# Which output tiles lend their buffers to the last two output pairs of a sliding-window attention and soft-MoE kernel

## The chip, the cores and the metric

The kernel runs on one core of one Trainium2 chip. The metric is device time in microseconds; before the change the median of 8 runs is 182.9 us (182.35 to 183.49).

A core has several engines that work side by side, each with its own queue of instructions in order: TensorE (PE, matmuls), VectorE (DVE), ScalarE (ACT), GpSimd (POOL) and SyncE (SP). The last two matter here mainly because they issue DMA transfers. An engine waits at the head of its queue until what its next instruction needs is there; whatever stands behind it waits too. The bytes of all transfers are moved by 16 DMA engines.

## The reference

An attention over 8 batches, 8 heads, 576 positions and head size 64 feeds a soft mixture of experts. Four heads see a plain window of 32 positions, the other four a window of 128 positions of which every fourth counts. The attention's result, 4608 rows of 512, is the input x of the mixture:

```python
logits = x @ phi                        # 4608 x 32 (8 experts x 4 slots)
d = softmax of logits over the rows     # dispatch
slot_input = d.T @ x                    # 32 x 512
h = relu(slot_input[e] @ w1[e])         # for each expert e, its 4 slots: 4 x 1024
slot_out[e] = h @ w2[e]                 # 4 x 512
c = softmax of logits over the slots    # combine
out = c @ slot_out                      # 4608 x 512, float32
```

The change lies in the last line alone: out = c @ slot_out and its way to memory.

## The kernel before

The attention and the statistics of the mixture run batch by batch, in an order written out by hand. At the end of that part the exponentials of all logits stand in a tile ET, with the 32 slots along the partitions, and the weights of the experts come in by DMA as the last input. The second part computes the experts and then the output.

**The output** is made in 36 blocks of 128 rows (NFIN), taken two at a time as 18 pairs. A block is one matmul of ET's columns with slot_out (so_sb), into a PSUM tile f; then ACT or DVE multiplies each row by the reciprocal of its sum of exponentials (rrow) on the way to an SBUF tile; then a DMA writes that to the output in device memory. There are three kinds of tile:

- *Halves*: pairs 0 to 7 are made in two column halves of 256 each, function `combine(half, pair)`. "Half 4" in this text is the second column half (half 1) of pair 4, "half 5" that of pair 5. An even pair is scaled by two ACT instructions (L774), an odd one by one DVE instruction (L778). The tile is float16, and POOL issues its DMA (L784), which casts to float32.
- *Full pairs* 8 to 15, `combine_full(pair)`: all 512 columns; the first block is scaled by ACT (L803), the second by DVE (L807), float16, and POOL issues the DMA (L814).
- *Full pairs* 16 and 17: the same, but scaled into float32, so that the DMA casts nothing, and it is SP that issues it (L814).

**Buffers.** SBUF is nearly full here, so some tiles take over a buffer that an earlier tile has held. The pool out_pool gives tiles of one tag the same buffers in turn; with one buffer to a tag, the next tile of that tag may be written when the DMA that reads the former one has landed. Seven second halves have buffers of their own under the tag ot1 (`bufs=NSPLIT // 2 - half`, 7). Two tags, last0 and last1, have one buffer each, of 128 x 2 x 512 float32. Before the change:

- last0: full pair 15 (float16, in the front of the buffer), then full pair 16
- last1: half 5 (float16, in the front of the buffer), then full pair 17

So the first instruction of full pair 16 (ACT, L803) waits until full pair 15's output has landed, and that of full pair 17 until half 5's has.

**Order.** The order of the instructions on every engine is the order in which the program writes them down (`manual_schedule`): full pairs 8 to 15, from pair 10 on each followed by one half (full 10, half 0, ... full 14, half 4, full 15, half 5), then halves 6 and 7, then full pairs 16 and 17. POOL's queue of issues is the same list up to half 7; SP's holds only pairs 16 and 17.

Of the kernel before, what the change touches and what calls it, by code (L numbers as in the profile page):

```python
# [9 lines left out]
FP32 = mybir.dt.float32  # L10
# [14 lines left out]
DMODEL = H * D  # L25
# [16 lines left out]
NFIN = N_ROWS // 128  # L42
# [7 lines left out]
def kernel(  # L50
# [607 lines left out]
    out_pool = tc.alloc_tile_pool(name="outp", bufs=1)  # L658
# [75 lines left out]
    def combine_one(half, blk):  # L734
        fp = psum_f.tile([128, NH], FP32, name=f"f{half}_one{blk}", tag="f")
        cols = slice(NH * half, NH * half + NH)
        r0 = 128 * blk
        nc.tensor.matmul(fp, ET[:, r0 : r0 + 128], so_sb[:, cols], start=True, stop=True)
        ot = out_pool.tile([128, NH], FP16, name=f"oo{half}_{blk}", tag=f"oo{half}_{blk}")
        if blk % 2 == 0:  # L740
            nc.scalar.activation(out=ot, in_=fp, func=AF.Copy, scale=rrow[:, blk : blk + 1])
        else:
            nc.vector.tensor_scalar(
                out=ot, in0=fp, scalar1=rrow[:, blk : blk + 1], scalar2=None, op0=ALU.mult
            )
        nc.gpsimd.dma_start(out=out[r0 : r0 + 128, cols], in_=ot)

    def combine(half, pair):
        if half == 0 and pair == 0:
            combine_one(half, 0)  # L750
            combine_one(half, 1)
            return
        fp = psum_f.tile([128, 2, NH], FP32, name=f"f{half}_{pair}", tag="f")
        r0 = 256 * pair
        for k in range(2):
            nc.tensor.matmul(
                fp[:, k, :],
                ET[:, r0 + 128 * k : r0 + 128 * k + 128],
                so_sb[:, NH * half : NH * half + NH],
                start=True,  # L760
                stop=True,
                skip_group_check=True,
            )
        if (half, pair) == (1, 5):
            ot = out_pool.tile([128, 2, DMODEL], FP32, name="last1_a", tag="last1")
            ot = ot[:, 0, 0:NH].bitcast(FP16).rearrange("p (k n) -> p k n", k=2)
        else:
            ot = out_pool.tile(
                [128, 2, NH], FP16, name=f"ot{half}_{pair}", tag=f"ot{half}", bufs=NSPLIT // 2 - half
            )  # L770
        if pair % 2 == 0:
            for k in range(2):
                blk = 2 * pair + k
                nc.scalar.activation(  # L774
                    out=ot[:, k, :], in_=fp[:, k, :], func=AF.Copy, scale=rrow[:, blk : blk + 1]
                )
        else:
            nc.vector.tensor_tensor(  # L778
                out=ot,
                in0=fp,  # L780
                in1=rrow[:, 2 * pair : 2 * pair + 2, None].broadcast_to([128, 2, NH]),
                op=ALU.mult,
            )
        nc.gpsimd.dma_start(  # L784
            out=out[r0 : r0 + 256, NH * half : NH * half + NH].rearrange("(k p) n -> p k n", k=2),
            in_=ot,
        )

    def combine_full(pair):
        r0 = 256 * pair  # L790
        if pair < NFIN // 2 - 3:
            ot = out_pool.tile([128, 2, DMODEL], FP16, name=f"of_{pair}", tag="of", bufs=6)
        else:
            tag = "last1" if pair == NFIN // 2 - 1 else "last0"
            ot = out_pool.tile([128, 2, DMODEL], FP32, name=f"ol_{pair}", tag=tag)
            if pair == NFIN // 2 - 3:
                ot = ot[:, 0, :].bitcast(FP16).rearrange("p (k n) -> p k n", k=2)
        for k in range(2):
            blk = 2 * pair + k
            fp = psum_f.tile([128, DMODEL], FP32, name=f"f_{blk}", tag="f")  # L800
            nc.tensor.matmul(fp, ET[:, 128 * blk : 128 * blk + 128], so_sb, start=True, stop=True)  # L801
            if k == 0:
                nc.scalar.activation(  # L803
                    out=ot[:, k, :], in_=fp, func=AF.Copy, scale=rrow[:, blk : blk + 1]
                )
            else:
                nc.vector.tensor_scalar(  # L807
                    out=ot[:, k, :],
                    in0=fp,
                    scalar1=rrow[:, blk : blk + 1],  # L810
                    scalar2=None,
                    op0=ALU.mult,
                )
        (nc.gpsimd if pair < NFIN // 2 - 2 else nc.sync).dma_start(  # L814
            out=out[r0 : r0 + 256, :].rearrange("(k p) n -> p k n", k=2), in_=ot
        )

    with tc.manual_schedule(engines=None):
        slot_out(0, ORDER[:6])
        slot_out(1, ORDER[:6])  # L820
        slot_out(0, HALVED)
        at = {5: 0}
        for pair in range(NSPLIT // 2):
            combine(0, pair)
            if pair in at:
                slot_out(1, (HALVED[at[pair]],))
        slot_out(1, HALVED[1:])
        for pair in range(NSPLIT // 2, NFIN // 2 - 2):
            combine_full(pair)
            if pair >= NFIN // 2 - NSPLIT // 2:  # L830
                combine(1, pair - (NFIN // 2 - NSPLIT // 2))
        for pair in range(2):
            combine(1, NSPLIT // 2 - 2 + pair)
        for pair in range(2):
            combine_full(NFIN // 2 - 2 + pair)
# [36 lines left out]
```

The softmax here doesn't subtract the row's maximum and nothing guards it: scores larger than these inputs give would overflow.

## Time and profile before

| what | value |
|---|---|
| median of 8 runs | 182.9 us (182.35 to 183.49) |
| the profiled execution, whole time | 183.03 us |
| its span, first to last instruction | 181.3 us |
| PE busy | 146.2 us (81%) |
| DVE, ACT, POOL busy | 107.3, 90.8, 83.7 us |
| the chain that ended last | DMA 41%, PE 34%, ACT 6%, POOL 6%, DVE 6% |
| read from and written to device memory | 61.93 MB, 9.44 MB |
| SP's two output transfers | 512 KB each, 1.05 MB together |

A profile comes from one execution. Its times count from the start of the span, in microseconds. The rows of digits cut the span into 40 equal slices, and a digit is the busy share in tenths. The row GB/s is what the 16 DMA engines moved. A line of the timeline has a start, a duration, the engine, the source line, the operation with the tiles it writes and reads, and in brackets how long the engine had been idle and what ended that. Tile names lose their numbers in it: `ol` is any of full pairs 15, 16 and 17, `ot` a half, `of` a full pair up to 14, and `last_a` is the half that sits in one of the two shared buffers. A row of a stretch has its length, the busy time (and the number of instructions) of PE, weight loads, DVE, ACT and POOL, then TensorE's clock, the DMA engines' mean busy share (over 1 where an engine has more than one packet in flight) and GB/s.

### The profile page before, as it was taken

To read this page: it belongs to the slowest core of one execution; us is meant where nothing else is said; L and a number is where in the kernel's file an instruction comes from. 1 tells how busy PE (TensorE), PEld (TensorE's weight loads), DVE (VectorE), ACT (ScalarE), POOL (GpSimd) and SP (SyncE) were. 2 spreads that over 40 slices of the span, in tenths; PEclk is the share of its full clock that TensorE was granted. 3 is DMA by queue.
4 is the path that set the end of the run, shared out by engine and by line. 5 is a ranking of instruction groups with operands and counts; after the bars stand their busy time and mean duration, and the time that the engine had idled before them with its cause. 6 is when DMAs were issued, how large, how long until landed. Compare 5 with 4: busy or idle time off the path is not lost.

```text
span 181.3 us, 5591 instructions
## 1 busy us (share of the span) xinstructions
PE 146.2 (81%) x2464; PEld 87.6 (48%) x2464; DVE 107.3 (59%) x232; ACT 90.8 (50%) x162; POOL 83.7 (46%) x124
## 2 busy tenths in 40 slices
PE   0467978999999999999999999998987986588000
PEld 0134445746655665664674674674735363233000
DVE  4689685876757676587598598443604024388030
ACT  2044454748555484765765765765430125497020
POOL 7954473633624163261444346334410443989700
PEclk9999995798589789789999999999755699889855
DMA  4999999999999999999999999999999999999996
GB/s 66 191 192 209 207 210 213 203 211 214 201 211 215 203 211 215 202 214 211 203 212 213 203 216 217 209 213 214 213 216 212 199 194 174 337 364 409 407 336 231
DMA packets 29527, 40.75 MB, mean 225 GB/s; under 512 B 1856, under 2 KB 19264, under 8 KB 29504
## 3 DMA queue, kind: packets, MB, share of 16 engines
q0 software_dynamic: 28960, 39.36, 116.1%
q1 hardware_dynamic: 544, 1.05, 1.6%
q8 instruction: 19, 0.31, 0.6%
q14 instruction: 4, 0.03, 0.0%
HBM read 61.93 MB, written 9.44 MB: 394 GB/s over the span
## 4 chain that ended last, share of the span: by engine, by line
DMA 41%; PE 34%; ACT 6%; POOL 6%; DVE 6%; issue 4%; DVEq 0%; POOLq 0%
DMA w<-in_moe_w_dram 28%; DMA raw<-in_k_dram 9%; ACT p L293 5%; PE lg L408 5%; PE o_p L339 4%; PE sa L282 4%; DMA out_dram<-ol 4%; PE sb L271 4%; PE sa L271 4%; PE rd L389 2%; DVE qk L245 2%; PE vb L163 2%; PE va L163 2%; PE u L452 2%; PE f L801 2%
## 5 line engine op out<-in xcount | busy, mean ns | idle before, releaser
L293 ACT ACTIVATE p<-sa 128x960 f16<-128x960 f32 (+2 forms) x24 | 21.4, 890 | 33.9 <-PE sb L282 33.3
L339 PEld LDWEIGHTS <-p 128*128 128x128 f16 (+2 forms) x544 | 19.7, 99 | 13.2 <-issue 9.0
L245 DVE STREAM_TRANSPOSE qk<-raw 128x320 uint32<-128x320 uint32 (+1 forms) x32 | 21.6, 679 | 0.3
L271 PE MATMUL sa<-masks,ident 128*128 128x480 f16 (+2 forms) x48 | 15.6, 414 | 7.3 <-POOL masks L489 6.2
L293 ACT ACTIVATE p<-sb 128x960 f16<-128x960 f32 (+2 forms) x24 | 21.2, 885 | 0.0
L236 DVE STREAM_TRANSPOSE qk<-raw 128x576 uint32<-128x576 uint32 x16 | 19.8, 1248 | 1.9 <-DMA raw<-in_k_dram 1.4
L271 PEld LDWEIGHTS <-ident 128*128 128x128 f16 x96 | 9.6, 112 | 18.9 <-issue 7.7
L282 PEld LDWEIGHTS <-qk 32*128 32x128 f16 x832 | 12.6, 101 | 12.0 <-issue 9.8
L408 PE MATMUL lg<-xTd,phi 128*128 128x288 f16 x32 | 18.3, 659 | 0.0
L339 PE MATMUL o_p<-v,p 128*128 128x65 f16 (+1 forms) x288 | 16.6, 202 | 1.2 <-ACT v L172 0.7
L282 PE MATMUL sa<-qk 32*128 32x160 f16 (+4 forms) x416 | 16.5, 218 | 0.8 <-DVE qk L236 0.7
L282 PE MATMUL sb<-qk 32*128 32x160 f16 (+4 forms) x416 | 16.5, 218 | 0.0
L209 POOL COPY v<-v 32x1024 f16<-32x1024 f16 x8 | 8.3, 1033 | 17.4 <-PE sb L282 10.3
L271 PE MATMUL sb<-masks,ident 128*128 128x480 f16 (+2 forms) x48 | 15.5, 411 | 0.5 <-ACT p L293 0.5
L212 POOL DMA_DIRECT2D w<-in_moe_w_dram x16 | 8.9, 556 | 14.6 <-DMA vs<-in_v_dram 6.6
L361 DVE TENSOR_TENSOR xp<-o_p,rc_p 128x448 f16<-128x448 f32 (+1 forms) x24 | 14.4, 602 | 0.9
L361 DVE TENSOR_TENSOR xd<-o_d,rc_d 128x448 f16<-128x448 f32 (+1 forms) x24 | 14.4, 602 | 0.8
L219 POOL DMA_DIRECT2D w<-in_moe_w_dram x10 | 6.7, 671 | 14.1 <-DMA w<-in_moe_w_dram 7.7
L412 ACT ACTIVATE ET<-lg 128x288 f16<-128x288 f32 x16 | 6.6, 410 | 12.6 <-PE lg L408 12.5
L163 PE MATMUL va<-vs,orders 32*128 32x256 f16 (+1 forms) x96 | 12.1, 290 | 0.9 <-ACT p L293 0.8
L360 DVE RECIPROCAL rc_p<-o_p 128x7 f32<-128x7 f32 (+1 forms) x24 | 4.7, 196 | 12.1 <-PE o_p L339 11.6
L382 ACT COPY xTp<-rp 128x576 f16<-128x576 f16 x16 | 10.4, 648 | 2.2 <-PE rp L377 2.2
(108 smaller groups left out, 277.8 us busy)
## 6 DMA issues: line engine op xcount, KB each, us to landing
w<-in_moe_w_dram POOLq DMA_DIRECT2D x16, 512.0 KB, 16.5
w<-in_moe_w_dram POOLq DMA_DIRECT2D x5, 1024.0 KB, 19.6
vs<-in_v_dram POOLq DMA_DIRECT2D x8, 512.0 KB, 14.3
raw<-in_q_dram POOLq DMA_DIRECT2D x7, 576.0 KB, 16.8
raw<-in_k_dram POOLq DMA_DIRECT2D x7, 576.0 KB, 17.1
out_dram<-ot POOLq DMA_DIRECT2D x14, 256.0 KB, 4.0
out_dram<-of POOLq DMA_DIRECT2D x7, 512.0 KB, 4.9
w<-in_moe_w_dram POOLq DMA_DIRECT2D x8, 256.0 KB, 9.6
```

Source lines behind the costliest of these rows:

```text
L163: nc.tensor.matmul(o.rearrange("p (h d) -> p h d", h=4), l, st[:, 0:4, D * r : D * r + D], start=(r == 0), stop=(r == DIL - 1), skip_group ...
L209: nc.gpsimd.tensor_copy(out=vL[b % NV][0:32, :, :, 0:D], in_=vD[b % NV][96:128, :, :, 0:D])
L212: nc.gpsimd.dma_start(out=w1t[e][:, 2 * i : 2 * i + 2, :].rearrange("p l f -> p (l f)"), in_=moe_w1[e, 256 * i : 256 * i + 256].rearrange( ...
L236: nc.vector.transpose(out=dst, in_=src)
L245: nc.vector.transpose(out=o, in_=i)
L271: nc.tensor.matmul(sps[h // 2][:, h % 2, 0:n], ident, bias[g], start=True, stop=False, skip_group_check=True,)
L282: nc.tensor.matmul(sps[h // 2][:, h % 2, c0 : c0 + w], kt_[32 * h : 32 * h + 32, k0 : k0 + 128, tt], qt_[32 * h : 32 * h + 32, q0 : q0 + w ...
L293: nc.scalar.activation(out=pt, in_=sps[ab][:, :, 0:n], func=AF.Exp, scale=SCALE)
L339: nc.tensor.matmul(o[p0 : p0 + np_, n, :], l, rr, start=(k == 0), stop=(k == len(jobs) - 1), skip_group_check=True,)
L361: nc.vector.tensor_tensor(out=x.rearrange("p t (h d) -> p (t h) d", h=4)[0:nq, u0:u1, :], in0=o[0:nq, 0:n, 0:D], in1=rc[0:nq, 0:n, None].b ...
L382: nc.scalar.copy(out=xTp_t[b][:, c, :], in_=rg)
L408: nc.tensor.matmul(lp, phi4[:, kc].rearrange("p c s -> p (c s)"), rhs, start=(kc == 0), stop=(kc == 3))
```

## The change

Half 4, not half 5, is put into one of the two shared buffers, and the tags of the full pairs are exchanged to match. After it:

- last0: half 4, then full pair 16
- last1: full pair 15, then full pair 17

Half 5 gets an ordinary buffer of the tag ot1, of which still seven are used. Nothing else differs: the order of instructions on each engine, their shapes and their number are the same.

```diff
-        if (half, pair) == (1, 5):
-            ot = out_pool.tile([128, 2, DMODEL], FP32, name="last1_a", tag="last1")
+        if (half, pair) == (1, 4):
+            ot = out_pool.tile([128, 2, DMODEL], FP32, name="last0_a", tag="last0")
             ot = ot[:, 0, 0:NH].bitcast(FP16).rearrange("p (k n) -> p k n", k=2)
         else:
             ot = out_pool.tile(
...
         if pair < NFIN // 2 - 3:
             ot = out_pool.tile([128, 2, DMODEL], FP16, name=f"of_{pair}", tag="of", bufs=6)
         else:
-            tag = "last1" if pair == NFIN // 2 - 1 else "last0"
+            tag = "last0" if pair == NFIN // 2 - 2 else "last1"
             ot = out_pool.tile([128, 2, DMODEL], FP32, name=f"ol_{pair}", tag=tag)
             if pair == NFIN // 2 - 3:
                 ot = ot[:, 0, :].bitcast(FP16).rearrange("p (k n) -> p k n", k=2)
```

## The prediction

> **What bounds the kernel now.** I began with the page's rows of time slices, to see what the last slices (4.53 us each) are made of.
>
> ```profile
> PE   0467978999999999999999999998987986588000
> ...
> DMA  4999999999999999999999999999999999999996
> GB/s 66 191 192 209 207 210 213 203 211 214 201 211 215 203 211 215 202 214 211 203 212 213 203 216 217 209 213 214 213 216 212 199 194 174 337 364 409 407 336 231
> ```
>
> TensorE is silent in the last three slices (from 167.7 us), while the DMA engines move about 400 GB/s. The tail is a drain of output; its last two slices show 336 and 231 GB/s, so something leaves the engines idle there. Next, the chain of work that ended last, its end (start us, us, what):
>
> ```profile
> 167.44 0.50 POOL out_dram L784
> 167.94 0.21 issue
> 168.15 6.94 DMA out_dram<-ol
> 175.22 0.50 DVE ol L807
> 175.71 0.09 issue
> 175.80 0.82 DVEq L867
> ```
>
> The step that matters is the DMA from 168.15 to 175.09: full pair 15's output, whose buffer (tag last0) full pair 16 needs. The timeline of 166.5 to 182 us gives the order of the steps around it:
>
> ```profile
> 167.43 0.72 POOL L784 DMA_DIRECT2D out_dram<-ot  x1
> 168.15 0.72 POOL L814 DMA_DIRECT2D out_dram<-ol  x1
> 168.86 0.72 POOL L784 DMA_DIRECT2D out_dram<-last_a  x1
> ...
> 175.19 1.26 ACT L803 ACTIVATE ol<-f,rrow 128x512 f32<-128x512 f32 x2 [8.65 <-DMA out_dram<-ol]
> 175.22 1.41 DVE L807 TENSOR_SCALAR ol<-f,rrow 128x512 f32<-128x512 f32 x2 [8.30 <-DMA out_dram<-ol]
> 176.04 1.04 SPq L814 DMA_DIRECT2D out_dram<-ol  x2
> ```
>
> The issues are, in order, half 4, full pair 15 and half 5. ScalarE and VectorE sat idle for 8.65 and 8.30 us until pair 15 landed; their matmuls had ended by 167.4 us. SP's first issue stands at 176.04 and, asked for alone, its second at 176.71. Landing times, from the DMA issues of three narrow windows (KB each, us from issue to landing):
>
> ```profile
> out_dram<-ot POOLq DMA_DIRECT2D x1, 256.0 KB, 6.3
> out_dram<-ol POOLq DMA_DIRECT2D x1, 512.0 KB, 6.9
> out_dram<-last_a POOLq DMA_DIRECT2D x1, 256.0 KB, 6.8
> ```
>
> So half 4 lands at 167.43 + 6.3 = 173.73, pair 15 at 168.15 + 6.94 = 175.09, half 5 at 168.86 + 6.8 = 175.66. The first two are 1.36 us apart, about what 512 KB take at 393 GB/s (1.33 us): the POOL queue lands in order at the rate of the bytes. Last, busy time by stretch, with DMA share and GB/s at the end of each row:
>
> ```profile
> 175.60:176.00 0.40, 0.00 (x0) 0.00 (x0) 0.40 (x2) 0.40 (x2) 0.00 (x0) 0.50 1.95 392
> 176.00:176.50 0.50, 0.00 (x0) 0.00 (x0) 0.50 (x1) 0.46 (x1) 0.00 (x0) 0.50 0.29 47
> 176.50:176.90 0.40, 0.00 (x0) 0.00 (x0) 0.12 (x1) 0.00 (x0) 0.00 (x0) 0.50 0.00 0
> 176.90:178.40 1.50, 0.00 (x0) 0.00 (x0) 0.00 (x0) 0.00 (x0) 0.00 (x0) 0.50 0.96 355
> 178.40:179.90 1.50, 0.00 (x0) 0.00 (x0) 0.00 (x0) 0.00 (x0) 0.00 (x0) 0.50 0.93 344
> ```
>
> This is the bound: the POOL queue runs dry at 176.0 (a straggle of 47 GB/s until about 176.45), nothing moves from 176.5 to 176.9, and SP's two outputs (1.05 MB) then run alone until about 179.8. In 100 ns stretches the first SP bytes come at 176.97, 0.93 us after the issue, and steady flow is near 391 GB/s.
>
> **The change part by part.**
>
> *Code and queues.* Every engine's instructions keep their order, count and shapes; no matmul, no DMA and no position in POOL's or SP's queue moves. Half 4 writes into the last0 buffer, half 5 into an ordinary one, pair 15 into last1. Half 4's ACT instructions (473 ns each) and half 5's DVE instruction (681 ns) only change address: cost 0. Neither new holder inherits a wait: last0 and last1 are fresh when first taken, and half 5's ordinary buffer is the one that half 4 gives up. What changes is two waits: full pair 16 waits for half 4 instead of pair 15, full pair 17 for pair 15 instead of half 5. Both new transfers were issued one POOL issue (0.72 us) earlier than the old ones. Queued behind the waiting ACT and DVE instructions is only pair 17's work, and behind that SP's two issues, so no other engine is held up.
>
> *Pair 16.* Released at 173.73 instead of 175.09. From release to SP's issue took 176.04 - 175.09 = 0.95 us (start-up 0.13, the DVE instruction 0.75, SP the rest), so the issue moves from 176.04 to 174.68, and first bytes from 176.97 to 174.68 + 0.93 = 175.61.
>
> *Pair 17.* Released at 175.09, when ACT and DVE have long finished pair 16 (173.86 + 0.75 = 174.61). Its issue is then at 175.09 + 0.95 = 176.04 instead of 176.71, its first bytes possible at 176.97. By then pair 16's bytes are still flowing, so it queues behind them and no gap opens.
>
> *What it is worth.* The release moves 1.36 us, but that isn't the gain: from 175.61 the POOL queue still has bytes to move, 0.40 us x 392 + 0.50 us x 47 = 180 KB, and pair 16 must share the engines with it. Total from there: 0.18 + 1.05 = 1.23 MB, at 391 GB/s 3.14 us, plus the ramp at both ends that SP's stretch shows now (1.05 MB would take 2.69 us at 391 and take 179.80 - 176.97 = 2.83: 0.14). Last byte at 175.61 + 3.14 + 0.14 = 178.89 instead of 179.80: 0.91 us gained.
>
> *The straggle.* From 176.05 to 176.45 only a few DMA engines still have POOL bytes. If each engine works off its own share, the latest has 0.4 us of backlog more than the mean and then its whole SP share: last byte at 179.3, a gain of 0.5. If SP's packets fill gaps of that engine, the straggle costs nothing. The trace has no stretch with bytes of both queues, so I cannot decide; I take half of it, 0.2 us, for a gain of 0.7. Bounds: 0.5 and 0.9 from the straggle; 1.3 if the queues together move more than either alone (near 450 GB/s); 0.2 if mixing costs some rate.
>
> *A rule that speaks against it.* The Trainium skill, DMA: Bandwidth & Descriptors, section "Issuing engines are not separate DMA queues", says that DMAs of all issuing engines end on the same 16 DMA engines and interleave. The row 175.60:176.00 (392 GB/s, POOL alone) against 178 to 179 us (391 GB/s, SP alone) agrees that SP's queue brings no rate of its own. Taken without a gap, the rule would give 0 for an earlier issue. The two rows after it show a gap: 0.9 us at 47 and then 0 GB/s, against about 350 KB possible at 391, of which 24 KB moved. Only this gap can be gained, 0.84 us, and with the slow first 0.1 us the 0.91 above. The same page, "Specifications", gives about 0.6 us to the first byte on this path; the trace has 0.93 and decides. With 0.6, pair 16 would start at 175.28, while the POOL queue is still at full rate: the total of bytes, and so the end, would be the same.
>
> *The frame.* After the last byte come the landing (180.26 to 180.3) and the closing semaphores to 181.3, both unmoved relative to the last byte. The profiled execution has span 181.3 and 183.03 us in all; 183.03 - 0.7 = 182.3. The median of the runs shown, 182.9, is 0.13 below it, so 182.2 for the median.
>
> **The rivals.**
>
> *A, the gap is filled (above).* 182.2, between 182.0 and 182.4 by the straggle.
>
> *B, filled without loss, and more.* If an engine moves more with two queues active, the overlap of some 0.9 us carries more: gain 1.0 to 1.3, 181.6 to 181.9. For it: the DMA share is 1.95 with POOL's packets and 0.96 with SP's at the same rate, so more packets in flight has not meant more bytes, which speaks against.
>
> *C, hidden.* The end doesn't move by more than 0.37 us, because mixing slows the overlap: 0.18 MB of POOL and as much of pair 16 take 0.92 us at 391 GB/s; at 260 GB/s they take 1.4, and with the straggle fully paid (0.4) the gain is 0.91 - 0.46 - 0.4, near 0: 182.9. For it: POOL's packets carry a cast and SP's don't, and no row shows them together. Against: the bytes' destination is the same memory, at one rate from either queue. That the change does nothing because half 4's landing isn't earlier is ruled out by 173.73 against 175.09, unless landings shift between executions.
>
> *D, slower.* The place is 175.6 to 177.5 us, the mechanism the mixing itself: each engine alternates between the two queues. It decides where the overlap's 0.36 MB take over 0.92 + 0.91 = 1.8 us, under 200 GB/s. At 150 GB/s they take 2.4 us, and the time is 183.5. Nothing in the profile speaks for half the rate; and pair 15's landing, on which pair 17 waits, lies at 175.09, before pair 16's first byte at 175.61, so this cannot delay the release.
>
> **How the numbers follow.** A 0.68, B 0.14, C 0.12, D 0.06. A measurement of this kernel tells a change of 0.2% (0.37 us) from none, so faster takes A and B, same takes C, slower D. The time is A's, 182.2. The range runs from B (181.7) to C's half with some gain left (182.7): a gain of 1.2 to 0.2.
>
> **What would show it right or wrong.** Right: ACT and DVE's first full-width f32 instructions start near 173.85, the second pair near 175.2; SP's issues at 174.7 and 176.05; no stretch below 300 GB/s between 175.6 and 178.5; last bytes at 178.9 to 179.3 and a span near 180.6. Step by step wrong: a start later than 174.2 (half 4's landing), SP later than 0.95 us behind the release, a rate under 300 GB/s from 175.6 to 177 (mixing, C or D), or an end set by one engine's tail (the straggle in full). Wrong altogether would be a span of 181.3 or more with SP's issue at 174.7: earlier bytes that don't help.

## The result and the profile after

The changed kernel takes 182.11 us (median of 20 runs, 181.51 to 183.54), the kernel before 182.88 us (55 runs, 182.21 to 183.63). The ratio is 0.9960, with a 95% interval from 0.9948 to 0.9972: 0.73 us less (the two medians lie 0.77 apart), between 0.5 and 0.95. The prediction had 182.2 us. A repetition beside the experiments below gave 0.9948 (0.9929 to 0.9968).

The profiled execution of the changed kernel has a span of 179.9 us and 181.59 us in all. It lies 0.5 us under its median, that of the kernel before 0.15 us over its own. Part of the difference between the two profiles therefore has nothing to do with the change: the last conversion of slot_out (so_sb, L730), behind which the whole tail lies, starts at 155.95 here and at 156.54 before. Counted from there to the end of the execution, the tail took 183.03 - 156.54 = 26.49 us before and 181.59 - 155.95 = 25.64 us after, 0.85 less. Times of different profiles are compared in this way below, or by differences within one profile.

The page's row of time slices (40 equal ones, here 4.50 us each) shows the same drain of output, with a fuller slice before the last: 399 GB/s in place of 336.

```profile
GB/s 63 197 194 209 208 209 212 206 208 217 200 211 215 202 212 213 203 211 211 206 211 211 210 207 216 212 212 217 210 215 212 204 195 184 307 393 408 412 399 217
```

The timeline of the changed kernel, from half 4's issue (`last_a` is now half 4):

```profile
166.15 0.72 POOL L784 DMA_DIRECT2D out_dram<-last_a  x1
167.21 0.72 POOL L814 DMA_DIRECT2D out_dram<-ol  x1 [0.35 <-issue]
...
173.20 0.69 ACT L803 ACTIVATE ol<-f,rrow 128x512 f32<-128x512 f32 x1 [8.18 <-DMA out_dram<-last_a]
173.24 0.75 DVE L807 TENSOR_SCALAR ol<-f,rrow 128x512 f32<-128x512 f32 x1 [7.85 <-DMA out_dram<-last_a]
174.06 1.64 SPq L814 DMA_DIRECT2D out_dram<-ol  x2
174.47 0.69 ACT L803 ACTIVATE ol<-f,rrow 128x512 f32<-128x512 f32 x1 [0.58 <-DMA out_dram<-ol]
174.49 0.75 DVE L807 TENSOR_SCALAR ol<-f,rrow 128x512 f32<-128x512 f32 x1 [0.50 <-DMA out_dram<-ol]
```

Two things are to be seen. Pair 16's first instructions are released by half 4's transfer, and pair 17's stand apart from them, released by pair 15's, 1.27 us later; before, all four ran in one go. SP's first issue is at 174.06, its second at 175.33. The rows of the DMA issues give the landings (KB each, us from issue to landing) of half 4 and pair 15:

```profile
out_dram<-last_a POOLq DMA_DIRECT2D x1, 256.0 KB, 7.0
out_dram<-ol POOLq DMA_DIRECT2D x1, 512.0 KB, 7.2
```

So half 4 lands at 166.15 + 7.0, about 173.1 (its last completion mark, explained further below, stands at 173.11), and pair 15 at 167.21 + 7.15 = 174.36. The end of the chain of work that ended last still names pair 15's transfer, since pair 17 is the last to be computed and waits for it:

```profile
167.21 7.15 DMA out_dram<-ol
```

That this wait no longer costs anything is not to be read from the chain; the experiments show it. The busy time by stretch shows what this did to the DMA engines (share and GB/s at the end of each row):

```profile
174.06:175.00 0.94, 0.00 (x0) 0.00 (x0) 0.51 (x1) 0.53 (x1) 0.00 (x0) 0.50 1.96 399
175.00:175.90 0.90, 0.00 (x0) 0.00 (x0) 0.24 (x1) 0.16 (x1) 0.00 (x0) 0.50 1.30 390
175.90:176.40 0.50, 0.00 (x0) 0.00 (x0) 0.00 (x0) 0.00 (x0) 0.00 (x0) 0.50 1.02 377
176.40:177.70 1.30, 0.00 (x0) 0.00 (x0) 0.00 (x0) 0.00 (x0) 0.00 (x0) 0.50 1.04 395
177.70:178.50 0.80, 0.00 (x0) 0.00 (x0) 0.00 (x0) 0.00 (x0) 0.00 (x0) 0.50 0.25 95
```

The stretch at 47 and 0 GB/s between the two queues is gone: the share falls from 1.96 to about 1 as SP's packets take over from POOL's, and the rate stays at 377 to 399 GB/s. In its place a weak stretch of 0.8 us at 95 GB/s stands at the very end, from 177.7 to 178.5, where the kernel before stopped within 0.2 us. The straggle, which stood ahead of the gap, has become the end of the kernel.

### The profile page after: what moved, and what is told of

Read it like the earlier page. It is cut to its first block, busy times and chain, and to the rows that moved or that the text cites. A ratio compares the mean times of both kernels' runs of the same rounds, so it can differ in the third digit from the quotient of the medians.

```text
span 179.9 us, 5591 instructions
## 1 busy us (share of the span) xinstructions
PE 143.1 (80%) x2464; PEld 85.4 (47%) x2464; DVE 107.0 (59%) x232; ACT 90.4 (50%) x162; POOL 83.8 (47%) x124
## 3 DMA queue, kind: packets, MB, share of 16 engines
q1 hardware_dynamic: 544, 1.05, 1.6%
## 4 chain that ended last, share of the span: by engine, by line
PE 52%; DMA 23%; ACT 10%; DVE 5%; POOL 4%; issue 3%; POOLq 0%; DVEq 0%
DMA w<-in_moe_w_dram 16%; PE lg L408 10%; ACT p L293 8%; PE o_p L339 7%; PE sa L282 7%; PE sb L271 5%; PE sa L271 5%; DMA out_dram<-ol 4%; PE u L452 3%; PE rd L389 3%; PE vb L163 3%; PE va L163 3%; DMA out_dram<-ot 3%; PE rp L377 2%; PE o_d L339 2%
## 5 line engine op out<-in xcount | busy, mean ns | idle before, releaser
L271 PE MATMUL sa<-masks,ident 128*128 128x480 f16 (+2 forms) x48 | 14.6, 390 | 7.3 <-POOL masks L489 6.2
L271 PEld LDWEIGHTS <-ident 128*128 128x128 f16 x96 | 9.1, 106 | 18.1 <-issue 7.2
L282 PEld LDWEIGHTS <-qk 32*128 32x128 f16 x832 | 12.1, 97 | 11.1 <-issue 8.9
L282 PE MATMUL sa<-qk 32*128 32x160 f16 (+4 forms) x416 | 16.0, 213 | 0.8 <-DVE qk L236 0.7
L271 PE MATMUL sb<-masks,ident 128*128 128x480 f16 (+2 forms) x48 | 14.3, 384 | 0.3 <-ACT p L293 0.2
L722 PE MATMUL so<-w,hTm 128*32 128x256 f16 x128 | 7.0, 349 | 5.0 <-DMA w<-in_moe_w_dram 4.1
```

The lines of the kernel that those rows point to most:

```text
L271: nc.tensor.matmul(sps[h // 2][:, h % 2, 0:n], ident, bias[g], start=True, stop=False, skip_group_check=True,)
L282: nc.tensor.matmul(sps[h // 2][:, h % 2, c0 : c0 + w], kt_[32 * h : 32 * h + 32, k0 : k0 + 128, tt], qt_[32 * h : 32 * h + 32, q0 : q0 + w ...
```

## The experiments

The theory: before the change, the end was set by the idle gap between POOL's last bytes and SP's first; the change is worth what of this gap is filled, and no more. Rivals: the earlier releases count by themselves; pair 17's own wait counts, since its output ends the kernel; bytes alone set the end; mixing two queues costs rate. All ratios are to the kernel before, run on the same chip beside each group.

**SP's issues exchanged.** The changed kernel's waits, with the early bytes taken away:

```diff
+    held = []
...
-        (nc.gpsimd if pair < NFIN // 2 - 2 else nc.sync).dma_start(
-            out=out[r0 : r0 + 256, :].rearrange("(k p) n -> p k n", k=2), in_=ot
-        )
+        held.append((pair, ot))
+        if pair == NFIN // 2 - 2:
+            return
+        for p, t in reversed(held):
+            r0 = 256 * p
+            (nc.gpsimd if p < NFIN // 2 - 2 else nc.sync).dma_start(
+                out=out[r0 : r0 + 256, :].rearrange("(k p) n -> p k n", k=2), in_=t
+            )
+        held.clear()
```

> The changed kernel with its two new waits kept, but SP's two issues exchanged: full pair 17's output is issued first, and full pair 16's behind it. So pair 16 is computed as early as in the changed kernel, and its bytes start no earlier than pair 17's. Theory (the gain is the idle gap of the DMA engines, filled by pair 16's early bytes): the gap is back, first SP bytes some 0.9 us behind an issue that now waits for pair 15's landing, just as before the change; ratio to the kernel before 1.000, within 0.002. Rival (the earlier releases of ACT and DVE are what counts): ratio 0.996, as for the whole change.

Measured: 182.86 us, ratio 0.9998 (0.9986 to 1.0010). The gain is gone. Its timeline has:

```profile
173.45 0.75 DVE L809 TENSOR_SCALAR ol<-f,rrow 128x512 f32<-128x512 f32 x1 [7.13 <-DMA out_dram<-last_a]
174.75 0.75 DVE L809 TENSOR_SCALAR ol<-f,rrow 128x512 f32<-128x512 f32 x1 [0.55 <-DMA out_dram<-ol]
175.57 0.92 SPq L821 DMA_DIRECT2D out_dram<-ol  x2
```

and its busy time by stretch:

```profile
175.00:175.50 0.50, 0.00 (x0) 0.00 (x0) 0.50 (x1) 0.41 (x1) 0.00 (x0) 0.50 2.00 408
175.50:176.50 1.00, 0.00 (x0) 0.00 (x0) 0.00 (x0) 0.00 (x0) 0.00 (x0) 0.50 0.43 81
```

Pair 16 is computed as early as in the changed kernel (DVE starts 17.26 us behind L730's start, there 17.29), but SP's first issue comes at 175.57, behind pair 17's computation, and the gap is back: 81 GB/s for one microsecond. Releasing ACT and DVE earlier is thus worth nothing; the early bytes are worth all of it.

**Pair 17 alone.** Full pair 17 takes over half 4's buffer, pair 16 still pair 15's:

```diff
-        if (half, pair) == (1, 5):
+        if (half, pair) == (1, 4):
             ot = out_pool.tile([128, 2, DMODEL], FP32, name="last1_a", tag="last1")
```

> One part alone: full pair 17 takes over half 4's buffer (landing about 1.9 us earlier than half 5), while full pair 16 still waits for pair 15 as before. Theory: pair 17 stands behind pair 16 on ACT, DVE and SP, and its bytes behind pair 16's, so nothing moves: 1.000, within 0.002. Rival (pair 17, whose output ends the kernel, sets the time by its own wait): 0.996 or less.

Measured: 183.02 us, ratio 1.0001 (0.9987 to 1.0015). Pair 17's new wait was long over when its turn came, and SP's first issue stayed where pair 16 put it, 19.47 us behind L730's start (19.50 in the kernel before). In this run half 4 already sits in a shared buffer and half 5 in an ordinary one, as in the changed kernel; that by itself is worth nothing either.

**Pair 16 alone.** Halves 4 and 5 lend their buffers, so pair 17 still waits for half 5; pair 15 moves into a seventh buffer of the full pairs:

```diff
-        if (half, pair) == (1, 5):
-            ot = out_pool.tile([128, 2, DMODEL], FP32, name="last1_a", tag="last1")
+        if half == 1 and pair in (4, 5):
+            n = pair - 4
+            ot = out_pool.tile([128, 2, DMODEL], FP32, name=f"last{n}_a", tag=f"last{n}")
...
-        if pair < NFIN // 2 - 3:
-            ot = out_pool.tile([128, 2, DMODEL], FP16, name=f"of_{pair}", tag="of", bufs=6)
+        if pair < NFIN // 2 - 2:
+            ot = out_pool.tile([128, 2, DMODEL], FP16, name=f"of_{pair}", tag="of", bufs=7)
```

> The other part alone: full pair 16 takes over half 4's buffer, full pair 17 still waits for half 5; pair 15 moves to an ordinary buffer of the full pairs (seven of these instead of six, and six of the second halves). Theory: pair 17's issue is about 0.6 us later than in the changed kernel, but pair 16's bytes still flow then, so the whole gain is there: 0.996, within 0.002. Rival (pair 17's wait carries the gain or half of it): 0.998 to 1.000.

Measured: 182.00 us, ratio 0.9952 (0.9936 to 0.9969): the whole gain. In its profile SP's second issue stands 1.92 us behind the first (176.35 and 174.43), against 1.27 in the changed kernel: 0.65 later, as expected. The rate dips to 245 GB/s from 176.2 to 177.3, so pair 17 is just late there; the time shows no cost of it (why not, is told in the next section). The whole change and this part of it cannot be told apart by their intervals.

**Both releases one step earlier.** As the run before, with halves 3 and 4 as lenders (`pair in (3, 4)`, `n = pair - 3`):

> Both releases one step earlier still: full pair 16 takes over half 3's buffer, full pair 17 half 4's; pair 15 in an ordinary buffer as in the run before. Pair 16 is released nearly 2 us earlier than in the changed kernel. Theory: the gap is already closed in the changed kernel and the engines have no rate to spare, so nothing more is gained: 0.996, within 0.002, and the DMA rate stays near 390 GB/s while both queues carry bytes. Rival (each us of earlier release is worth most of a us): 0.988 or less. Second rival (mixing the two queues for longer costs rate): above 0.998.

Measured: 181.88 us, ratio 0.9947 (0.9926 to 0.9968). To see whether it is ahead of the changed kernel, both were run side by side:

> The run with half 3 and half 4 as lenders once more, beside the changed kernel on the same chip. Theory (gap closed, no more to gain): the same as the changed kernel, both 0.995 to 0.997. Rival: 0.2% or more below it.

> The changed kernel itself, beside the run before: 0.996, within 0.0015.

Measured: 182.17 us, 0.9966 (0.9952 to 0.9980), and for the changed kernel 181.79 us, 0.9948 (0.9929 to 0.9968). Against the first measurement of the changed kernel (0.9960) this version looked a little ahead; side by side it is a little behind. No difference between the two is shown. From the timeline of this version (the run with 181.88 us):

```profile
171.41 0.75 DVE L806 TENSOR_SCALAR ol<-f,rrow 128x512 f32<-128x512 f32 x1 [4.68 <-DMA out_dram<-last_a]
172.24 2.39 SPq L813 DMA_DIRECT2D out_dram<-ol  x2
```

Counted from L730, SP's first issue is 2.0 us earlier than in the changed kernel, and the last packet of its output only 0.15 us earlier. What became of the earlier issue is told by the rows of the DMA queues (packets, MB, busy share of 16 engines; q0 carries POOL's transfers, q1 SP's). The first row is all that ran from 174 to 175 us, the other two are from 175.5 to 176:

```profile
q0 software_dynamic: 409, 0.39, 194.9%
...
q1 hardware_dynamic: 68, 0.14, 77.7%
q0 software_dynamic: 77, 0.06, 69.3%
```

SP's first packet starts at 175.55, 3.31 us behind its issue (0.92 us in the changed kernel), when POOL's packets begin to run out; the last of these ends at 175.96. In the repeated run the wait is 2.93 us. So the longer time between issue and gap did not make the two queues share the engines for longer: SP's packets stood behind POOL's. A release is worth something only until the gap is closed.

**Two halves left out.** Halves 6 and 7 are neither computed nor written, in the kernel before and in the changed one:

```diff
-        for pair in range(2):
-            combine(1, NSPLIT // 2 - 2 + pair)
```

> The kernel before with the second halves of pairs 6 and 7 left out: they are neither computed nor written, 0.52 MB of output and 1.3 us of the DMA engines less. Nothing waits for them in the program. Theory (before the change the end is set by pair 15's landing and not by bytes): the POOL queue runs dry 1.3 us earlier, the idle gap grows by that, and the time stays: 1.000, within 0.003. Rival (the drain of bytes sets the end): 1.3 us less, 0.993.

> The changed kernel with the same two halves left out. Theory: the POOL queue now ends at about 174.9, before SP's first bytes at about 175.6, so a gap of some 0.7 us opens again; SP's bytes then run alone, with no backlog on single engines, and end 1.36 us before those of the kernel before, as early as the release of pair 16 was moved: 0.9925, within 0.002 (181.5). Rival (bytes count one for one in either kernel): 0.996 less 1.3 us, 0.989. The spread of pair 17's landing over the 16 DMA engines should fall from 0.8 us in the changed kernel to some 0.25.

Measured: the kernel before without them 182.86 us, ratio 1.0001 (0.9988 to 1.0014); the changed kernel without them 181.44 us, 0.9924 (0.9907 to 0.9941). Of the first of them, SP's issues in the timeline:

```profile
175.78 1.04 SPq L814 DMA_DIRECT2D out_dram<-ol  x2
```

and its busy time by stretch:

```profile
174.00:175.00 1.00, 0.00 (x0) 0.00 (x0) 0.04 (x1) 0.06 (x1) 0.00 (x0) 0.50 0.50 96
175.00:176.00 1.00, 0.00 (x0) 0.00 (x0) 1.00 (x2) 1.00 (x2) 0.00 (x0) 0.50 0.00 0
```

Half a megabyte less to write changed nothing before the change: the engines only idle longer (no packet of output runs from 175.08 to 176.72, against 176.53 to 176.98 with all halves). That is the clearest sign that not bytes but pair 15's landing set the end. With the new buffers the full 1.36 us of the earlier release appear once there is idle time to take them from: 182.88 - 181.44 = 1.44, by the interval between 1.1 and 1.7. A gap is left there too, from 174.81 to 175.26.

## Why the prediction was right

**The releases.** ACT and DVE start on pair 16 behind half 4's landing and on pair 17 behind pair 15's, as worked out. From landing to SP's issue were 0.95 us; here half 4 landed at 173.11 and the issue is at 174.06, again 0.95. The two releases lie 1.27 us apart for the 1.36 expected.

**The first bytes.** Expected 0.93 us behind the issue. SP's first packet starts at 174.98, 0.92 us behind 174.06. The figure of about 0.6 us in the Trainium skill (DMA: Bandwidth & Descriptors, "Specifications") was again not what this kernel shows.

**No rate of its own.** The rule that was weighed against the change, that all queues share the same 16 engines, agrees with every run; only the gap could be gained, estimated at 0.84 to 0.91 us less the straggle. Both halves of this are shown: with early bytes taken away nothing is gained, and with a still earlier release nothing more. That the queues also interleave, as the same section has it, was not to be seen: with halves 3 and 4 as lenders no packet of SP's ran for 3.31 us after its issue while POOL's did. It looks as if each DMA engine first works off what POOL's queue has given it. The packets in the trace carry no engine number, so this is not shown engine by engine. Rival B (more than the gap) is ruled out by the time. C and D (mixing costs rate) are ruled out for this change: while packets of both queues run, from 175.0 to 175.9, the rate is 390 GB/s. What a long mixing would cost stays open, since none took place.

**The straggle was mis-sized, and taking half of it was luck.** For lack of a row I took 0.2 us, the middle of two cases. One of them came true, but with a term of the wrong size. The packets of the output (the pieces in which the DMA engines move it, 2 KB each in SP's transfers) settle it, in us from the start of L730:

```
                            POOL's last   SP's first   SP's last     SP's last
                            packet ends   packet       packet ends   behind POOL's
before                         19.98        20.43        23.35          3.37
SP's issues exchanged          19.87        20.30        23.22          3.35
pair 17 alone                  19.95        20.39        23.31          3.36
changed                        19.98        19.03        22.55          2.57
changed, repeated              19.97        19.02        22.53          2.57
pair 16 alone                  19.97        19.04        22.54          2.57
halves 3 and 4 as lenders      19.82        19.41        22.39          2.57
the same, repeated             19.89        18.99        22.46          2.57
```

Wherever SP's packets are there in time, the output ends 2.57 us behind POOL's last packet, however early the release; with the gap it is 3.35 to 3.37. So the straggle counts in full, as in the case that was to gain 0.5 us: it seems that the engine which is last with POOL's bytes sets the end. An end set by one engine's tail was among the prediction's signs of a wrong step.

But that case gave this engine 2.69 + 0.14 = 2.83 us for its share of SP's output, a time read behind a gap, and it needs 2.57. Of the 0.80 us between 3.37 and 2.57, the gap itself is 0.45 (20.43 - 19.98); the other 0.35 is a shorter drain. Behind a gap SP's packets take 2.90 to 2.92 us from first to last, in all five profiles that have one. The errors nearly cancel: in the times of the kernel before, the end comes to 176.53 + 2.57 = 179.10, and 178.89 + 0.2 = 179.09 was forecast. Why the drain is shorter without a gap ahead of it is open; nothing was run on it.

How far the other engines are ahead does not count. A transfer here leaves 16 completion marks; the same page of the Trainium skill, section "Why a DMA increments its semaphore by 16 and not by 1", has each DMA engine that takes part give one. At half 7 the latest mark lies 0.40 us behind the median before and 0.81 in the changed kernel, where it is still 0.70 behind at pair 17. With halves 3 and 4 as lenders the lag at pair 17 is 0.28 in one profile and 0.71 in the other, with pair 16 alone 0.20, and all three end 2.57 us behind POOL's last packet. So with pair 16 alone, the dip in the rate seems to have been idle time of engines that were ahead. An idle gap takes the lag away: in the kernel before without halves 6 and 7 it falls from 0.81 at half 5 to 0.11 at pair 17. Why a few engines lag is open.

**What was not needed.** That pair 17's wait was moved too turned out to be worth nothing that can be measured: alone it gives 1.0001, and without it the gain is whole.

## What to carry to other kernels

When the tail of a kernel is a drain of output over two DMA queues, look for the time between the last bytes of the one and the first bytes of the other; it costs the end directly, however busy the engines look on average. To find what an earlier release is worth, don't count by how much the release moves, but by how much idle time of the DMA engines it can fill. A last transfer that waits for a landed buffer should borrow it from a transfer that lands early enough to close the gap; borrowing from a still earlier one brings nothing.

## What was not expected of the hardware

An earlier issue on SP's queue did not bring its packets in among POOL's: issued 3.31 us ahead, they began only when POOL's ran out. And 1.05 MB of SP's output took 2.90 to 2.92 us when it followed an idle gap, but ended 2.57 us behind POOL's last packet in all five runs without one. Closing a gap of 0.45 us therefore returned about 0.8 us in the profiles (0.73 by the runs' ratio): the gap between the last packets of the one queue and the first of the other was only a part of its cost.
